# Memory attention and two layers of experts on one core: the prologue rearranged (loads, weight decoding, sums of phi, place of batch 1's attention)

## The chip, the cores and the metric

The kernel runs on one core of a Trainium2 chip. A core has a matrix engine (PE, TensorE), a vector engine (DVE), a scalar engine (ACT), GpSimd (POOL) and a sequencer for DMA issues (SP); each works through its own list of instructions in order, and semaphores tie the lists together. The time is that of one execution on the device, in microseconds (us); the median of three runs counts.

## The reference

```python
# attention with memory: 8 batches, 8 heads, 576 tokens, 64 dims, 32 slots
a = exp(phi - max(phi, axis=2)); a = a / (sum(a, axis=2) + 1e-9)
k_m = einsum('bhsm,bhsd->bhmd', a, k); v_m = einsum('bhsm,bhsd->bhmd', a, v)
scores = q @ k_m^T / sqrt(64)
attn = exp(scores - max(scores)); attn = attn / (sum(attn) + 1e-9)
x = (attn @ v_m), rows of 8 heads x 64            # 4608 x 512
# first layer, weights in float64
h = maximum(maximum(x @ w1, x @ w2), x @ w3)      # 512 -> 768
x = h @ w_out                                     # 768 -> 512
# second layer: of 8 experts the one with the largest logit of x @ w_gate
out = gate_w * (maximum(x @ w1[e], 0) @ w2[e])
```

## The kernel before

The work goes through eight batches. **Attention** of batch b (the `at_` functions) loads phi, k, v and q; takes the maximum of phi over the tokens (`at_max` along the free axis, `at_col` across partitions with a transpose on PE, tile `ps_mx`, then `mc` and `mb`), subtracts it (`at_sub`), takes the exponential on ACT (`at_exp`) and the sum (`at_asum`), and multiplies by k and v on PE (`at_km`, 72 small matmuls, tile `ps_kv`). `kx` and `vx` are the products divided by the sum; `at_kvT` transposes them on PE, `at_qT` transposes q on DVE, `at_scores` makes 32 matmuls, and `at_smax`, `at_sexp`, `at_ssum`, `at_out` are the softmax by halves of the heads (`par`), with the result split into `at_hi` and `at_lo`.

**First layer.** Values are kept as a high part, rounded to the type the fast matmul takes, and the rest: ACT makes the first, DVE or POOL the second (`split`, L94 and L95), and a product is three matmuls (`mm3`, L98 to L100). v_m is folded into the weights: `u_step(b, f)` multiplies a block of `w123` by vT and splits it. `m1_step(b, f, hf, i)` multiplies it by at (6 matmuls of 288 columns); over i, the three products are joined by a maximum `hx` on DVE (L418), and split, `h_lo` on POOL. With 6 f, 2 hf, 3 i these are 216 matmuls in a batch. `m2_step(b, d, hf)` multiplies by w_out, 18 matmuls each, 8 of them in a batch, and needs all six f of h. After it come the gate (`gate_a` to `gate_c`), and at the end, the experts.

**Weights.** The float64 weights of the first layer come in 24 parts (18 of `w123`, 6 of w_out, 128 x 512 words of 8 bytes, 512 KB). `decode_a` takes the upper word's absolute value on ACT (L138) and clamps it (L141); `decode_b` does three bit operations on DVE (L148, L151, L154). A part of w_out is split besides, `wo_lo` on POOL. Parts 0, 1, 2, 8, 11, 15, 22 and 23 are clamped on DVE, the others on POOL. Four raw buffers (`w64`) hold what was loaded.

**Order.** The program is written with a list of times: `attention(b+1)` returns steps with due times (`AT`, and `AT1` for batch 1), and `stream.advance` runs those that are due as m1 and m2 steps of batch b go by; `start_step` decodes the next part in batch 0. A scheduler then fixes the order on each engine. SP issues all loads in one queue in that order. TensorE starts with 34 warm-up matmuls.

Of the kernel before, what the change touches and what calls it, by code (L numbers as in the profile page):

```python
# [19 lines left out]
def kernel(  # L20
# [141 lines left out]
    def w_load(n):  # L162
# [3 lines left out]
        if isinstance(part, tuple):  # L166
            f, i = part
            t = sp.tile([P, J, P], U64, tag="w64", name="w64", bufs=4)
# [27 lines left out]

    def at_max(b):
        t = inp["phi", b]
        mx = ep.tile([P, J, M], F32, tag="mx", name="mx")
        nc.vector.tensor_reduce(out=mx, in_=t.rearrange("p j c m -> p j m c"), axis=AX.X, op=ALU.max)  # L200
        st["mx", b] = mx

    def at_col(b):
# [7 lines left out]
        nc.vector.tensor_copy(out=mb, in_=mc.to_broadcast([P, 2, HP]))  # L211
# [15 lines left out]
    def at_asum(b):  # L227
        t = inp["phi", b]
        asum = ep.tile([P, J, M], F32, tag="mx", name="asum")
        nc.vector.tensor_reduce(out=asum, in_=t.rearrange("p j c m -> p j m c"), axis=AX.X, op=ALU.add)  # L230
        st["asum", b] = asum

    def at_km(b):

        t, kv = inp["phi", b], inp["kv", b]
        pss = [ps_at.tile([P, 512], F32, tag="at", name="ps_kv") for _ in range(2)]
# [11 lines left out]
        for par in range(2):  # L248
# [187 lines left out]

# [330 lines left out]
    with ExitStack():  # L767
        on_dve = (0, 1, 2, 8, 11, 15, 22, 23)

        def w_clamp(n):  # L770
# [4 lines left out]
        load_kv(0, 1)
        w_load(0)
        for j in range(J):
            load_q(0, j)
        w_load(1)
        w_load(2)  # L780
        w_load(3)
        nc.sync.dma_start(out=wg[:, :, 0:E], in_=w_gate.rearrange("(d p) e -> p d e", p=P))
# [17 lines left out]
        w_done(2)  # L800
        w_done(1)
        at_qT(0, 0)
        at_qT(0, 1)
# [1 line left out]
        at_qT(0, 2)
        at_qT(0, 3)
        at_scores(0)
        at_smax(0, 0)
        at_sexp(0, 0)
        w_clamp(3)  # L810
        w_done(3)
        w_clamp(4)
        at_smax(0, 1)
        at_sexp(0, 1)
        at_ssum(0, 1, nc.gpsimd)
        at_ssum(0, 0)
        at_out(0, 0)
        w_done(4)
        at_out(0, 1)
        w_clamp(5)  # L820
# [181 lines left out]
```

## Time and profile before

| | us |
|---|---|
| median of three runs | 1017.89 (1017.39 to 1018.23) |
| the profiled execution | 1020.95 |
| its span | 1019.2 |
| PE busy, DVE, ACT, POOL | 974.2, 580.4, 355.0, 180.5 |
| last at_lo of batch 0 done | 54.6 |
| first matmul of batch 0's m2 | 102.7 |
| first matmul of batch 1's m1 | 130.66 |

The busy times of the engines are sums over the span, which has stages with different limits: the first attention with nothing to hide it, the decoding of the weights beside batch 0's m1, and then seven batches and the experts. So the profile is read by stage. "PEclk" is the clock that was granted to TensorE as a share of full speed (1.0 is 2.4 GHz, 0.5 is 1.2 GHz). A duration in the timeline overlaps the next instruction's by some hundredths of a microsecond, so that the distance from start to start is a little shorter than the duration; for a matmul of 288 columns it is 0.13 where the row says 0.29.

### The profile page before, as it was taken

The page shows a single profiled execution, that of the slowest core. Times are in us where ns is not written, and L with a number is a line of the kernel's source. Part 1 is how long each engine was busy: PE and PEld are TensorE (multiplying, and loading weights), DVE is VectorE, ACT ScalarE, POOL GpSimd, SP SyncE. Part 2 cuts the span into 40 slices and gives each one's busy share as a digit, 9 for nine tenths or more (in the row PEclk, how much of TensorE's full clock was granted, in tenths as well). Part 3 has the DMA queues.
Part 4 walks back from the last instruction along what each step waited for, and adds up shares of the span by engine and source line. Part 5 has one row for each costly group of instructions (what it writes and reads, how often), then busy time and mean ns, then how long its engine had stood idle before and what let it go on. Part 6 is the DMA issues. An engine that isn't in the chain of part 4 may idle for free. (4 is left out here: it accounts for less than half of the span.)

```text
span 1019.2 us, 20430 instructions
## 1 busy us (share of the span) xinstructions
PE 974.2 (96%) x8296; PEld 854.4 (84%) x8296; DVE 580.4 (57%) x1257; ACT 355.0 (35%) x732; POOL 180.5 (18%) x294
## 2 busy tenths in 40 slices
PE   5498899999999999999999999999999999999997
PEld 5176788879888798888989989898989898989886
DVE  5989968385683846838256717171717172626341
ACT  2344433333333434333346406060605050504130
POOL 0124212011120111202121121212121211111110
PEclk7589899999999999999999999999999999999999
DMA  8828214132041321210108517161616161625030
GB/s 313 281 84 277 67 58 161 52 118 70 25 164 48 118 78 37 98 48 2 47 18 267 189 32 223 36 219 41 215 41 201 53 206 51 197 63 155 21 109 22
DMA packets 59105, 114.78 MB, mean 113 GB/s; under 512 B 7687, under 2 KB 20999, under 8 KB 59008
## 3 DMA queue, kind: packets, MB, share of 16 engines
q1 hardware_dynamic: 48480, 94.01, 27.8%
q0 software_dynamic: 4768, 9.94, 4.2%
q10 hardware_dynamic: 5760, 9.48, 2.5%
q8 instruction: 67, 1.10, 0.4%
q14 instruction: 30, 0.25, 0.1%
HBM read 94.00 MB, written 19.44 MB: 111 GB/s over the span
## 5 line engine op out<-in xcount | busy, mean ns | idle before, releaser
L98 PE MATMUL ps_m<-at_hi,u_hi 128*128 128x288 f32 x576 | 178.9, 312 | 3.0 <-DVE hx L418 2.0
L100 PE MATMUL ps_m<-at_hi,u_lo 128*128 128x288 f32 x576 | 170.6, 297 | 2.4 <-DVE u_lo L95 2.4
L99 PE MATMUL ps_m<-at_lo,u_hi 128*128 128x288 f32 x576 | 170.8, 297 | 0.8 <-DVE at_lo L95 0.8
L98 PE MATMUL ps_x<-yh,w1h 128*128 128x288 f32 (+1 forms) x544 | 160.2, 295 | 0.1
L99 PE MATMUL ps_x<-yl,w1h 128*128 128x288 f32 (+1 forms) x544 | 159.9, 294 | 0.0
L100 PE MATMUL ps_x<-yh,w1l 128*128 128x288 f32 (+1 forms) x544 | 159.9, 294 | 0.0
L95 POOL TENSOR_TENSOR h_lo<-hx,h_hi 128x288 fp32r<-128x288 f32 x96 | 83.8, 873 | 375.7 <-ACT h_hi L94 375.6
L98 PEld LDWEIGHTS ps_m<-at_hi,u_hi 128*128 128x128 f32 x576 | 108.6, 189 | 36.6 <-issue 21.5
L596 POOL DMA_DIRECT2D out_dram<-o x144 | 70.9, 499 | 345.6 <-DVE o L593 306.2
L418 DVE TENSOR_TENSOR hx<-hx,ps_m 128x288 f32<-128x288 f32 x192 | 85.2, 446 | 74.5 <-PE ps_m L100 50.6
L98 PE MATMUL ps_m<-h_hi,wo_hi 128*128 128x288 f32 x384 | 115.8, 302 | 1.6 <-ACT wo_hi L94 1.6
L100 PE MATMUL ps_m<-h_hi,wo_lo 128*128 128x288 f32 x384 | 114.1, 298 | 1.3 <-POOL wo_lo L95 1.3
L99 PE MATMUL ps_m<-h_lo,wo_hi 128*128 128x288 f32 x384 | 114.3, 298 | 0.0
L100 PEld LDWEIGHTS ps_m<-at_hi,u_lo 128*128 128x128 f32 x576 | 108.7, 189 | 4.3 <-DVE u_lo L95 3.1
L99 PEld LDWEIGHTS ps_m<-at_lo,u_hi 128*128 128x128 f32 x576 | 109.1, 189 | 2.4 <-issue 1.2
L593 DVE TENSOR_SCALAR o<-ps_x,scal 128x512 f32<-128x512 f32 x32 | 24.0, 751 | 151.6 <-PE ps_x L100 151.6
L98 PE MATMUL ps_x<-w2h,xh 128*128 128x512 f32 x272 | 107.7, 396 | 0.0
L99 PE MATMUL ps_x<-w2l,xh 128*128 128x512 f32 x272 | 107.5, 395 | 0.0
L100 PE MATMUL ps_x<-w2h,xh 128*128 128x512 f32 x272 | 107.4, 395 | 0.0
L98 PEld LDWEIGHTS ps_x<-yh,w1h 128*128 128x128 f32 x544 | 102.0, 188 | 1.4 <-PE ps_g L443 0.5
L99 PEld LDWEIGHTS ps_x<-yl,w1h 128*128 128x128 f32 x544 | 102.1, 188 | 0.5 <-ACT yl L682 0.2
L100 PEld LDWEIGHTS ps_x<-yh,w1l 128*128 128x128 f32 x544 | 102.1, 188 | 0.0
(177 smaller groups left out, 1593.5 us busy)
## 6 DMA issues: line engine op xcount, KB each, us to landing
raw<-in_moe_w_dram SPq DMA_DIRECT2D x72, 512.0 KB, 4.5
raw<-y_dram SPq DMA_DIRECT2D x36, 288.0 KB, 3.1
kv_t<-in_k_dram SPq DMA_DIRECT2D x8, 1152.0 KB, 7.7
kv_t<-in_v_dram SPq DMA_DIRECT2D x8, 1152.0 KB, 9.7
w<-in_moe_w_dram SPq DMA_DIRECT2D x18, 512.0 KB, 4.0
q_t<-in_q_dram SPq DMA_DIRECT2D x32, 288.0 KB, 3.0
y_dram<-y_sb ACTq DMA_DIRECT2D x32, 288.0 KB, 2.1
out_dram<-o POOLq DMA_DIRECT2D x144, 64.0 KB, 1.9
```

What stands on the lines that cost most here:

```text
L95: eng.tensor_tensor(out=dst_lo, in0=src, in1=dst_hi, op=ALU.subtract)
L98: nc.tensor.matmul(out=ps, lhsT=hi_l, rhs=hi_r, start=first, stop=False)
L99: nc.tensor.matmul(out=ps, lhsT=hi_l, rhs=lo_r, start=False, stop=False)
L100: nc.tensor.matmul(out=ps, lhsT=lo_l, rhs=hi_r, start=False, stop=last)
L418: nc.vector.tensor_tensor(out=hx[0], in0=hx[0], in1=ps, op=ALU.max)
L593: nc.vector.tensor_scalar(out=o, in0=ps, scalar1=scal[:, b, t:t + 1], scalar2=None, op0=ALU.mult)
L596: nc.gpsimd.dma_start(out=out5[b, half, c], in_=o[i:i + TB])
```

## The change

- **Loads.** phi, two parts of weights and k go first, then w_gate. The other early loads are tied to a point of the computation by `after`: ACT writes one element of the target from a finished tile, and the load must follow it. w2 and v follow `mb`, w3, the four q and w4 the exponential, two more parts follow `vx`. Six raw buffers in place of four. Part 6 is asked for twice, once by name and once by `w_done(0)`.
- **Decoding.** All clamps on DVE, and `wo_lo` too; of POOL's work in the prologue only `h_lo` stays. `at_ssum`'s product of batch 0 moves to DVE as well.
- **phi.** The maximum, and the sum from batch 2 on, as four tensor_tensor over halves of the chunks (`over_chunks`). The sums of batches 0 and 1 are 72 matmuls against ones. `mb`, `kx` and `vx` are written by ACT.
- **Batch 1's attention** is due late in batch 0 (`AT1`), and its loads follow parts 14, 15 and 17. `start_step` runs at four of six m1 steps.
- **m2 of batch 0, first half**, goes by rows of w_out: four PSUM tiles at once, f as the outer loop. Batch 1's first two `u_step` come in the second half.

```diff
+    NRAW = 6
-    AT1 = dict(max=5, col=8, sub=10, q=(20, 22, 23.5, 25), exp=12.5, asum=13.5, km=24.5, kvT=28.5, sc=31.5,
-               smax=(33, 36), sexp=(36, 38.5), ssum=(37.5, 43), out=(41, 46))
+    AT1 = dict(max=22, col=24, sub=26, q=(24, 25, 26, 27), exp=28, asum=29, km=33, kvT=35, sc=38,
+               smax=(40, 41), sexp=(41, 42.5), ssum=(43, 45), out=(46, 48))
...
+    def after(t, src):
+        nc.scalar.activation(out=t[0:1], in_=src, func=AF.Copy)
...
-        eng.tensor_scalar(out=dst, in0=dst, scalar1=F64_MAX, scalar2=F64_MIN, op0=ALU.min, op1=ALU.max)
+        nc.vector.tensor_scalar(out=dst, in0=dst, scalar1=F64_MAX, scalar2=F64_MIN, op0=ALU.min, op1=ALU.max)
...
-            split(wo_hi[:, part], wo_lo[:, part], wdst[n], nc.gpsimd)
+            split(wo_hi[:, part], wo_lo[:, part], wdst[n])
...
+    def over_chunks(dst, t, op):
+        h = ep.tile([P, J, 4, M], F32, tag="hc", name="hc")
+        nc.vector.tensor_tensor(out=h, in0=t[:, :, 0:4], in1=t[:, :, 4:8], op=op)
+        nc.vector.tensor_tensor(out=h[:, :, 0:2], in0=h[:, :, 0:2], in1=h[:, :, 2:4], op=op)
+        nc.vector.tensor_tensor(out=dst, in0=h[:, :, 0], in1=t[:, :, 8], op=op)
+        nc.vector.tensor_tensor(out=dst, in0=dst, in1=h[:, :, 1], op=op)
...
-        nc.vector.tensor_reduce(out=mx, in_=t.rearrange("p j c m -> p j m c"), axis=AX.X, op=ALU.max)
+        over_chunks(mx, t, ALU.max)
...
-        nc.vector.tensor_copy(out=mb, in_=mc.to_broadcast([P, 2, HP]))
+        nc.scalar.activation(out=mb, in_=mc.to_broadcast([P, 2, HP]), func=AF.Copy)
...
+        if b < 2:
+            pss = st["kvp", b] = [ps_at.tile([P, 512], F32, tag="at", name="ps_kv") for _ in range(2)]
...
+                            lhsT=t[r0:r0 + HP, j, c, :],
+                            rhs=ones[r0:r0 + HP, 0:1],
...
-        nc.vector.tensor_reduce(out=asum, in_=t.rearrange("p j c m -> p j m c"), axis=AX.X, op=ALU.add)
+        over_chunks(asum, t, ALU.add)
...
-            nc.vector.tensor_scalar(out=vx[:, par], in0=ps[:, D:2 * D], scalar1=r, scalar2=None, op0=ALU.mult)
+            nc.scalar.activation(out=vx[:, par], in_=ps[:, D:2 * D], func=AF.Copy, scale=r)
...
+    def m2_by_f(b, hf):
+        pss = [m2_tile(b, d, hf) for d in range(ND)]
+        for f in range(NF1):
+            for d in range(ND):
+                m2_part(b, pss[d], d, hf, f)
+        for d in range(ND):
+            m2_end(b, pss[d], d, hf)
...
-        on_dve = (0, 1, 2, 8, 11, 15, 22, 23)
...
+        w_load(2, st["mb", 0][0:1, 0, 0:1])
+        load_kv(0, 1, st["mb", 0][0:1, 0, 0:1])
...
+        gone = inp["phi", 0][0:1, J - 1, 0, 0:1]
+        w_load(3, gone)
+        for j in range(J):
+            load_q(0, j, gone)
+        w_load(4, gone)
...
+        w_load(5, st["kx", 0][1][0:1, 1, 0:1])
+        w_load(6, st["kx", 0][1][0:1, 1, 0:1])
...
-                stream.add([(0, lambda: load_phi(1)), (20, lambda: load_kv(1, 0)), (21.5, lambda: load_kv(1, 1))])
-                stream.add([(4 + 1.5 * j, lambda j=j: load_q(1, j)) for j in range(J)])
+                stream.add([(16, lambda: load_phi(1, done(14)))])
+                stream.add([(17 + j, lambda j=j: load_q(1, j, done(15))) for j in range(J)])
+                stream.add([(22 + i, lambda i=i: load_kv(1, i, done(17))) for i in range(2)])
...
-                        if b == 0 and (hf, i) in ((0, 0), (1, 0), (1, 2)):
+                        if b == 0 and i != 1:
                             start_step()
...
+                if b == 0 and hf == 0:
+                    m2_by_f(b, hf)
```

**DVE between the first maximum of batch 0 and its subtraction.** `w` is a part of the weights, `qT` a transposed block of q. Before:

```order
L200 TENSOR_REDUCE mx<-phi_t 128x128
L289 STREAM_TRANSPOSE qT<-q_t 128x576 x2
L141 TENSOR_SCALAR w_96<-w_96 128x512
L289 STREAM_TRANSPOSE qT<-q_t 128x576
L148 TENSOR_SCALAR w_96<-w_96 128x512
L289 STREAM_TRANSPOSE qT<-q_t 128x576
L151 SCALAR_TENSOR_TENSOR w_96<-w_153,w_96 128x512
L209 TENSOR_REDUCE mc<-ps_mx 128x2
L154 SCALAR_TENSOR_TENSOR w_96<-w_153,w_96 128x512
L211 COPY mb<-mc 128x128
L141 TENSOR_SCALAR w_96<-w_96 128x512
L218 TENSOR_TENSOR phi_t<-phi_t,ps_mb 128x1152
```

Now (L213 to L216 are the maximum by halves, L152, L159, L162 and L165 what L141, L148, L151 and L154 were):

```order
L215 TENSOR_TENSOR mx<-hc,phi_t 128x128
L216 TENSOR_TENSOR mx<-mx,hc 128x128
L152 TENSOR_SCALAR w_96<-w_96 128x512
L159 TENSOR_SCALAR w_96<-w_96 128x512
L152 TENSOR_SCALAR w_96<-w_96 128x512
L162 SCALAR_TENSOR_TENSOR w_96<-w_150,w_96 128x512
L159 TENSOR_SCALAR w_96<-w_96 128x512
L165 SCALAR_TENSOR_TENSOR w_96<-w_150,w_96 128x512
L162 SCALAR_TENSOR_TENSOR w_96<-w_152,w_96 128x512
L165 SCALAR_TENSOR_TENSOR w_96<-w_152,w_96 128x512
L230 TENSOR_REDUCE mc<-ps_mx 128x2
L239 TENSOR_TENSOR phi_t<-phi_t,ps_mb 128x1152
```

Two parts are decoded ahead of the column maximum `mc`, and nothing stands between it and the subtraction; the four transposes of q come later.

**PE around the end of batch 0's m1.** `ps_kvT` and `ps_sc` are batch 1's transposes and scores, `h_hi,wo_hi` is m2. Before, they stand inside m1:

```order
L98 MATMUL ps_m_1033<-at_hi,u_hi 128x288
L99 MATMUL ps_m_1033<-at_lo,u_hi 128x288
L98 MATMUL ps_m_1052<-at_hi,u_hi 128x288
L99 MATMUL ps_m_1052<-at_lo,u_hi 128x288
L278 MATMUL ps_kvT<-ident,kx 128x128 x2
L279 MATMUL ps_kvT<-ident,vx 128x128
L302 MATMUL ps_sc<-qT,kT 32x288
L100 MATMUL ps_m_1033<-at_hi,u_lo 128x288
L98 MATMUL ps_m_1033<-at_hi,u_hi 128x288
```

Now they stand behind the 72 matmuls of m2 by rows, of which these are the last:

```order
L99 MATMUL ps_m_1265<-h_hi,wo_hi 128x288
L100 MATMUL ps_m_1265<-h_lo,wo_hi 128x288
L101 MATMUL ps_m_1265<-h_hi,wo_lo 128x288
L314 MATMUL ps_kvT<-ident,kx 128x128 x2
L315 MATMUL ps_kvT<-ident,vx 128x128
L99 MATMUL ps_m_1409<-h_hi,wo_hi 128x288
L100 MATMUL ps_m_1409<-h_lo,wo_hi 128x288
L101 MATMUL ps_m_1409<-h_hi,wo_lo 128x288
L99 MATMUL ps_m_1409<-h_hi,wo_hi 128x288
L338 MATMUL ps_sc<-qT,kT 32x288 x32
```

So kvT and scores of batch 1 moved from m1 to behind m2's first half; the sum (L257) and km (L277) stand just ahead of m2.

**PE at batch 1's first m1 block.** Each `ps_m` reads `at_hi` and `at_lo` twice, first for one half of the heads, then for the other. Before:

```order
L100 MATMUL ps_m_1356<-h_hi,wo_lo 128x288
L98 MATMUL ps_m_1377<-at_hi,u_hi 128x288
L99 MATMUL ps_m_1377<-at_lo,u_hi 128x288
L100 MATMUL ps_m_1377<-at_hi,u_lo 128x288
L98 MATMUL ps_m_1377<-at_hi,u_hi 128x288
L99 MATMUL ps_m_1377<-at_lo,u_hi 128x288
L100 MATMUL ps_m_1377<-at_hi,u_lo 128x288
L98 MATMUL ps_m_1390<-at_hi,u_hi 128x288
L99 MATMUL ps_m_1390<-at_lo,u_hi 128x288
```

Now:

```order
L101 MATMUL ps_m_1519<-h_hi,wo_lo 128x288
L99 MATMUL ps_m_1540<-at_hi,u_hi 128x288
L100 MATMUL ps_m_1540<-at_lo,u_hi 128x288
L101 MATMUL ps_m_1540<-at_hi,u_lo 128x288
L99 MATMUL ps_m_1540<-at_hi,u_hi 128x288
L99 MATMUL ps_m_1553<-at_hi,u_hi 128x288
L100 MATMUL ps_m_1553<-at_lo,u_hi 128x288
L101 MATMUL ps_m_1553<-at_hi,u_lo 128x288
L99 MATMUL ps_m_1553<-at_hi,u_hi 128x288
L99 MATMUL ps_m_1567<-at_hi,u_hi 128x288
L100 MATMUL ps_m_1567<-at_lo,u_hi 128x288
L100 MATMUL ps_m_1540<-at_lo,u_hi 128x288
```

The first product with `at_lo` of the second half, `ps_m_1377<-at_lo` the second time and now `ps_m_1540<-at_lo` the second time, was the fifth matmul of the block and is now the eleventh. From the next block on, PE's list is the same in both.

## Rows read from the trace of the kernel before

**Rows 1.** Stages: us, busy (x) PE PEld DVE ACT POOL, PEclk, DMA share, GB/s.

```profile
0.00:12.70 12.70, 9.50 (x69) 9.27 (x69) 2.70 (x13) 1.94 (x2) 0.70 (x6) 1.00 0.86 320
12.70:35.50 22.80, 11.07 (x209) 6.17 (x220) 21.36 (x42) 7.62 (x14) 3.10 (x5) 0.62 0.88 291
35.50:54.60 19.10, 10.27 (x70) 4.46 (x57) 19.08 (x34) 5.95 (x10) 3.22 (x4) 0.50 0.67 233
54.60:102.70 48.10, 43.53 (x482) 33.34 (x481) 44.29 (x83) 22.04 (x47) 19.24 (x22) 0.95 0.59 197
102.70:130.70 28.00, 25.09 (x179) 22.12 (x178) 25.08 (x41) 10.67 (x22) 6.12 (x5) 0.88 0.27 86
130.70:1019.20 888.50, 874.73 (x7307) 779.09 (x7306) 467.92 (x1047) 306.76 (x638) 148.16 (x253) 1.00 0.31 99
```

**Rows 2.** Timeline of PE at batch 1's first m1 block: start us, us, instruction.

```profile
130.53 0.29 PE L100 MATMUL ps_m<-h_hi,wo_lo 128*128 128x288 f32 x1
130.66 0.29 PE L98 MATMUL ps_m<-at_hi,u_hi 128*128 128x288 f32 x1
```

**Rows 3.** Timeline of DVE, phi of batch 0; [idle before <-releaser].

```profile
4.83 2.16 DVE L200 TENSOR_REDUCE mx<-phi_t 128x128 f32<-128x1152 f32 x1 [3.33 <-DMA phi_t<-in_phi_dram]
18.30 1.35 DVE L218 TENSOR_TENSOR phi_t<-phi_t,ps_mb 128x1152 f32<-128x1152 f32 x1 [0.23 <-PE ps_mb L217]
```

**Rows 4.** Timeline of DVE in the weight decoding.

```profile
68.33 0.68 DVE L151 SCALAR_TENSOR_TENSOR w<-w,w 128x512 uint32<-128x512 uint32 x1
68.93 0.44 DVE L418 TENSOR_TENSOR hx<-hx,ps_m 128x288 f32<-128x288 f32 x1
69.29 0.93 DVE L154 SCALAR_TENSOR_TENSOR w<-w,w 128x512 uint32<-128x512 uint32 x1
72.69 0.42 DVE L148 TENSOR_SCALAR w<-w 128x512 uint32<-128x512 uint32 x1
73.49 0.92 DVE L141 TENSOR_SCALAR w<-w 128x512 f32<-128x512 f32 x1
```

**Rows 5.** Timeline of DVE, the last at_lo of batch 0 and of batch 1.

```profile
53.88 0.75 DVE L95 TENSOR_TENSOR at_lo<-aT,at_hi 128x576 fp32r<-128x576 f32 x1
126.50 0.70 DVE L95 TENSOR_TENSOR at_lo<-aT,at_hi 128x576 fp32r<-128x576 f32 x1
```

**Rows 6.** The page's DMA issues: KB each, us from issue to landing.

```profile
w<-in_moe_w_dram SPq DMA_DIRECT2D x18, 512.0 KB, 4.0
```

**Rows 7.** Windows of two microseconds: us, PE busy (x), PEclk, DMA share, GB/s.

```profile
4.00:6.00 2.00, 2.00 (x17) 1.00 1.06 412
104.00:106.00 2.00, 0.59 (x3) 1.00 0.10 39
108.00:110.00 2.00, 1.30 (x6) 0.50 0.00 0
```

**Rows 8.** Timeline of ACT, exp of phi of batch 0.

```profile
19.69 1.26 ACT L225 ACTIVATE phi_t<-phi_t 128x576 f32<-128x576 f32 x2 [1.17 <-DVE phi_t L218]
```

**Rows 9.** Timeline of PE, attention products of batches 0 and 1.

```profile
20.43 4.64 PE L241 MATMUL ps_kv<-kv_t,phi_t 64*32 64x128 f32 x144 [2.16 <-ACT phi_t L225]
29.42 0.66 PE L278 MATMUL ps_kvT<-ident,kx 128*128 128x128 f32 x2 [4.00 <-DVE kx L267]
33.33 4.16 PE L302 MATMUL ps_sc<-qT,kT 32*32 32x288 f32 x62
85.22 1.56 PE L241 MATMUL ps_kv<-kv_t,phi_t 64*32 64x128 f32 x92
98.82 1.45 PE L302 MATMUL ps_sc<-qT,kT 32*32 32x288 f32 x46
```

**Rows 10.** Lines of DVE, 0 to 135: busy us, mean ns | idle before.

```profile
L151 DVE SCALAR_TENSOR_TENSOR w<-w,w 128x512 uint32<-128x512 uint32 x18 | 14.4, 805 | 0.1
```

**Rows 11.** Timeline of POOL beside the clamp at 73.49.

```profile
73.32 0.80 POOL L95 TENSOR_TENSOR h_lo<-hx,h_hi 128x288 fp32r<-128x288 f32 x1 [3.66 <-ACT h_hi L94]
```

**Rows 12.** Waits of PE, 131 to 1020: us, times, longest.

```profile
PE ps_m L98 <- DVE hx L418: 2.0, 6, 0.3
```

More of the change, by code (lines that the diff above doesn't have):

```diff
@@ L160, with w_load @@
     wraw, wdst = {}, {}
-    def w_load(n):
+    def w_load(n, src=None):
         if n >= len(wparts):
@@ L167, in w_load @@
             f, i = part
-            t = sp.tile([P, J, P], U64, tag="w64", name="w64", bufs=4)
+            t = sp.tile([P, J, P], U64, tag="w64", name="w64", bufs=NRAW)
+            if src is not None:
+                after(t.bitcast(F32)[:, 0, 0:1], src)
             nc.sync.dma_start(
@@ L228, in at_asum @@
         t = inp["phi", b]
+        if b < 2:
+            pss = st["kvp", b] = [ps_at.tile([P, 512], F32, tag="at", name="ps_kv") for _ in range(2)]
+            for c in range(NCH):
+                for j in range(J):
+                    for par in range(2):
+                        r0 = HP * par
+                        nc.tensor.matmul(
+                            out=pss[par][32 * j:32 * j + 32, 2 * D:2 * D + 1],
+                            lhsT=t[r0:r0 + HP, j, c, :],
+                            rhs=ones[r0:r0 + HP, 0:1],
+                            start=(c == 0),
+                            stop=(c == NCH - 1),
+                        )
+            return
         asum = ep.tile([P, J, M], F32, tag="mx", name="asum")
-        nc.vector.tensor_reduce(out=asum, in_=t.rearrange("p j c m -> p j m c"), axis=AX.X, op=ALU.add)
+        over_chunks(asum, t, ALU.add)
         st["asum", b] = asum
@@ L235, in at_km @@
         t, kv = inp["phi", b], inp["kv", b]
-        pss = [ps_at.tile([P, 512], F32, tag="at", name="ps_kv") for _ in range(2)]
+        pss = st.pop(("kvp", b)) if b < 2 else [ps_at.tile([P, 512], F32, tag="at", name="ps_kv") for _ in range(2)]
         for c in range(NCH):
@@ L247, in at_km @@
                     )
-        for par in range(2):
+        for par in range(2) if b >= 2 else ():
             r0 = HP * par
@@ L767 @@
     with ExitStack():
-        on_dve = (0, 1, 2, 8, 11, 15, 22, 23)
-        def w_clamp(n):
-            w_a(n, nc.vector if n in on_dve else nc.gpsimd)
         load_phi(0)
+        w_load(0)
+        w_load(1)
         load_kv(0, 0)
[L775 to L782, printed above, removed]
         def w_done(n):
+            w_a(n)
             w_b(n)
-            w_load(n + 4)
+            if n + NRAW < len(wparts) and n + NRAW not in wraw:
+                w_load(n + NRAW)
         at_max(0)
         at_col(0)
+        w_load(2, st["mb", 0][0:1, 0, 0:1])
+        load_kv(0, 1, st["mb", 0][0:1, 0, 0:1])
         at_sub(0)
@@ L793 @@
         at_asum(0)
-        w_clamp(0)
-        w_clamp(1)
+        gone = inp["phi", 0][0:1, J - 1, 0, 0:1]
+        w_load(3, gone)
+        for j in range(J):
+            load_q(0, j, gone)
+        w_load(4, gone)
+        w_done(0)
+        w_done(1)
+        w_done(2)
         at_km(0)
-        w_done(0)
-        w_clamp(2)
+        w_load(5, st["kx", 0][1][0:1, 1, 0:1])
+        w_load(6, st["kx", 0][1][0:1, 1, 0:1])
         at_kvT(0)
[L800 to L803, printed above, removed]
-        u_step(0, 0)
[L805 to L820, printed above, removed]
+        nc.sync.dma_start(out=wg[:, :, 0:E], in_=w_gate.rearrange("(d p) e -> p d e", p=P))
+        for j in range(J):
+            at_qT(0, j)
+        w_done(3)
+        w_done(4)
+        at_scores(0)
+        u_step(0, 0)
+        for p in range(2):
+            at_smax(0, p)
+            at_sexp(0, p)
         w_done(5)
-        w_clamp(7)
-        w_clamp(6)
+        for p in range(2):
+            at_ssum(0, p)
+            at_out(0, p)
         u_step(0, 1)
@@ L872 @@
             for hf in range(2):
+                if b == 0 and hf == 0:
+                    m2_by_f(b, hf)
                 for d in range(ND):
[L874 removed]
+                    if b > 0 or hf > 0:
+                        m2_step(b, d, hf)
                     stream.advance(2.25)
[L876 to L877 removed]
+                    if b + 1 < B and (hf, d) in (((0, 2), (1, 1)) if b else ((1, 1), (1, 2))):
+                        u_step(b + 1, (hf, d) == ((1, 1) if b else (1, 2)))
             stream.rest()
```

61 lines of the change are left out of this document (32 added, 29 removed).

## The prediction

> **What bounds the kernel now.** I read the page's busy shares first, then the windows by stage, then the timelines of single engines inside each stage. TensorE is busy for 974.19 of the 1019.2 us of the span, but not evenly. From 130.70 us on it is busy for 874.73 of 888.50 us at clock 1.00 [rows 1]. Up to there it is not: 12.70 to 54.60 is batch 0's attention, on a half-empty TensorE at a clock of 0.62 and then 0.50, and 54.60 to 130.70 is weight decoding beside batch 0's first products. In these two stages VectorE is the bound: 21.36 of 22.80 us, 19.08 of 19.10, 44.29 of 48.10, 25.08 of 28.00 [rows 1]. The change touches this prologue and little else. In both programs TensorE's order is the same from batch 1's first m1 block to the end, so the result is nearly **one number: when TensorE reaches that block**, 130.66 us before [rows 2].
>
> All sums are in the time of the profiled execution, 1020.95 us, of which 1019.2 is span. It lies 3.06 above the median 1017.89; I add differences to the median. A difference under 0.2%, 2.0 us, can't be told from no change.
>
> **First stage, to the scores of batch 0.** Before, phi's first maximum starts at 4.83 and takes 2.16, but its subtraction only ran at 18.30 [rows 3]: the column maximum stood on VectorE behind a part of a weight and four transposes of q. In the new order these come later. The maximum by halves is four tensor_tensor of 512, 256, 128 and 128 columns. A line through 288 columns (0.36 from start to start) and 576 (0.70 and 0.75 long, about 0.66 from start to start) [rows 4, 5] gives 0.60 + 0.33 + 0.20 + 0.20 = 1.3. ps_mx still waits for the warm-up matmuls, which held TensorE until about 10.6; column maximum, copy (on ScalarE now) and transpose bring the subtraction to about 12.6, 5.7 earlier.
>
> Most of that is lost to transfers. w2 and v are now held back until the copy mb, at about 12.4. A part of a weight lands 4.0 after its issue [rows 6], so w2 at 16.4; v (1152 KB at the 412 GB/s of [rows 7]) lands 2.9 after it, at 19.3. ScalarE's exp, 1.26 for both halves [rows 8], ends at about 15.3. Then come the 72 matmuls against ones that replace the reduction asum. No row has them; the nearest is the km product, 144 passes in 4.64 at half clock, 32 ns each [rows 9]. As many passes cost 4.6, 15.3 to 19.9. Below they could cost a third if one column is cheaper than 128, but then v's landing is next, so the value hardly moves km: it starts at 19.9 and ends at 24.5, where before it ran 20.43 to 25.07. What helps next is the queue on VectorE: kx came 4.00 after TensorE had stopped [rows 9], and it now runs on ScalarE, to about 27.0. Scores then run 28.2 to 32.5 where they ran 33.33 to 37.49 [rows 9]: **5.0 gained**. The softmax of batch 0 and what stands between takes 15.8 on VectorE by the new order (35 instructions, the rows of one price each), against 17.1 before; so the last at_lo ends at T0 = 48.3, before 54.63 [rows 5]: **6.3 gained**. If the scores run at full clock (46 passes in 1.45 instead of 62 in 4.16 [rows 9]), T0 is 46.3.
>
> **Second stage, T0 to phi(1)'s subtraction.** VectorE now does all clamps (16 are left here), wo_lo and phi(1)'s maximum. By its order: 16 clamps at 0.34 = 5.4, 15 L159 at 0.34 = 5.1, 15 L162 and 17 L165 at 0.60 = 19.2 (from start to start in a clean run, 0.42 and 0.68 long [rows 4]), 18 hx at 0.365 = 6.6, six u_lo at 0.47 = 2.8, five wo_lo at 0.60 = 3.0, the maximum 1.3, mc 0.2, the subtraction 1.3, two qT at 0.70 = 1.4: **46.3**.
>
> To this comes contention. Before, L151 took 805 ns on average and 0.68 in the clean run [rows 4, 10], and a clamp that met h_lo on GpSimd took 0.92 instead of 0.42 [rows 4, 11]. Of GpSimd's work only h_lo remains, about nine in this stretch; at 0.35 each 3.2, between 0 and 0.50 each = 4.5. And TensorE's waits come back to VectorE as waits for hx; of the 3.8 idle of before (48.10 - 44.29 [rows 1]) I keep 1.1. So the stage takes 50.6 and the subtraction ends at S = 98.9.
>
> The Trainium skill, "SBUF — State Buffer", section "🔬 SBUF: two separate sides", says of the port pair that VectorE and GpSimd share that it is an exclusive lock: who comes second stands still for the other's whole instruction. The clamp of [rows 4, 11] agrees: 0.92 ends 0.3 after the 0.80 of h_lo does. By that rule nine h_lo could cost 9 x 0.80 = 7.2, and the total would be 4.0 above mine.
>
> **Third stage, S to batch 1's m1.** This is what the change adds. Before, batch 1's attention was spread through the decoding: phi(1)'s sum and km lay among m1 blocks, kvT and the scores too, and all were hidden. Now they stand at the end, in a chain. After S: exp 1.5 [rows 8], 72 matmuls against ones at 17 ns a pass (92 in 1.56 [rows 9]) = 2.45, 32 matmuls of m1 at 0.133 (130.53 to 130.66 [rows 2]) = 4.3, km 2.45: w_out's rows begin at M = S + 10.7 = **109.6**. They began at 102.7 before, but at half clock and with gaps. Then m2 by rows, 72 x 0.133 = 9.6, which stands ahead of kvT on TensorE; kvT 0.5, four matmuls 0.5, scores 64 x 31.5 ns = 2.0. Behind these the softmax of batch 1 on VectorE, with nothing to hide it but the other half of m2: four transposes at 0.40, twelve operations on 576 columns and four qT at 0.68, sums and two u_lo 1.5, exp's latency 0.3 = 14.3. Thus at_lo of the second half is there at M + 26.9 = 136.5, while TensorE's own filler ends at M + 23.5. In the new order the matmul that needs it is the eleventh of batch 1; before, it would have stood at 130.66 + 10 x 0.133 = 132.0. **Lag: 4.5 us.**
>
> **Later batches.** Maximum and sum by halves take 1.3 instead of 2.16 and 2.2; VectorE is not the bound there, but TensorE waits 2.0 for hx in six places [rows 12]. Some of that goes: 0.3 in five batches, 1.5; bounds 0 and 2.0. The moves of mb, kx, vx to ScalarE cost nothing there, since ScalarE is busy for 306.76 of 888.50 [rows 1]. The w_load of part 6 is issued twice, 1.3 us of transfers at 412 GB/s; it delays part 7 on the queue, and six raw buffers cover it.
>
> Forecast: 1017.89 + 4.5 - 1.5 = 1020.9, **1021.0**.
>
> **Rivals.**
> *The prologue sheds its idle time (faster).* Scores at full clock (T0 2.0 earlier), no contention left (3.2), no waits (1.1): M is 103.3, the lag -1.8, and with 2.0 from the later batches the time is 1014; with the softmax tail one or two us shorter, down to 1010.5. For it: VectorE's excess over clean durations was some 7 us in the second stage and GpSimd's part in it goes. Against: h_lo stays, and the clean durations are already in my sum. It decides below M = 105.
>
> *The clock falls in the thin stage (slower).* TensorE's work from T0 to S is 216 matmuls at 0.133 = 28.7 and some 5 for u, of 50.6. Before, a gap at 104 to 106 with 0.59 busy was followed by a clock of 0.50 at 108 to 110, for some microseconds [rows 7]. The stage from 102.70 has a mean clock of 0.88 [rows 1], which over 28.00 us is one spell of some 6.8 at half clock. If such a spell falls on the chain from S to the scores it costs 3.4, twice 6.8: 1024 to 1028, typically 1027. It decides if TensorE idles just ahead of S, while it waits for phi(1). The Trainium skill, "TensorE: Matmul & The Clock Gate", section "HAM oscillation — how this bites in real kernels", has bursts of matmuls divided by waits start each time at the low clock; that speaks against this change, which makes bursts of the chain, and by it the upper of these times would hold.
>
> *What is gained is given back exactly.* The 6.3 of the first stage pay for the tail, M is near 106.3 and nothing can be measured: 1018.
>
> *The lock of the whole instruction* in the second stage (contention 7.2 instead of 3.2): 1025. The row of the clamp bears it out once; most of VectorE's instructions there don't meet an h_lo. I give it 0.08, inside the forecast's share.
>
> **How the numbers follow.** Forecast, with its own range 1017.0 to 1025.0: 0.41 (slower 0.29, same 0.11, faster 0.01). Idle shed: 0.32 (faster 0.31, same 0.01). Clock: 0.19, all slower. Given back: 0.08 (same 0.06, faster 0.01, slower 0.01). Sums: faster 0.33, same 0.18, slower 0.49. The range runs from the far end of the first rival, 1010.5, to beyond the clock's two spells, 1029.5; outside I leave 1 in 10 on either side.
>
> **What would show it.** Right: the subtraction at 12 to 13, scores of batch 0 ended by 33, T0 47 to 49, S near 99, m2's first matmul at 108 to 111, VectorE idle for some 20 us between S and batch 1's scores, a wait of TensorE of about 3 us for at_lo just ahead of batch 1's m1, and that block at 134 to 137. Wrong in the gain: S under 94. Wrong in the clock: granted clock 0.5 anywhere from 85 to 125. Wrong altogether: a shift of batch 1's m1 that is not the shift of the end.

## The result, and the profile after

The changed kernel took 1033.45 us (median of four runs, 1031.11 to 1035.3) beside 1018.06 before: a ratio of **1.0148, interval 1.0122 to 1.0175, slower**. The forecast was 1021.0, range 1010.5 to 1029.5: the right side, and 12 us too low. The profiled execution of the changed kernel has a span of 1033.0, 13.8 more than before.

The stages of the profile after, cut where VectorE begins phi(1)'s subtraction (100.7), where m2 begins (117.2) and where batch 1's m1 begins (142.5); columns as in [rows 1]:

```profile
0.00:12.70 12.70, 9.68 (x70) 9.44 (x70) 6.55 (x25) 3.05 (x5) 0.70 (x6) 1.00 0.67 223
12.70:32.50 19.80, 8.71 (x325) 6.44 (x326) 10.20 (x21) 6.61 (x23) 0.00 (x0) 0.65 0.81 280
...
49.50:100.70 51.20, 37.63 (x236) 28.12 (x234) 48.47 (x100) 22.00 (x52) 11.92 (x8) 0.83 0.62 209
100.70:117.20 16.50, 13.81 (x322) 11.36 (x323) 8.32 (x19) 4.25 (x10) 2.40 (x3) 0.59 0.22 59
117.20:142.50 25.30, 24.32 (x245) 21.01 (x244) 15.49 (x31) 8.55 (x21) 0.80 (x1) 1.00 0.54 188
142.50:1032.00 889.50, 874.44 (x7308) 779.17 (x7306) 458.54 (x1053) 312.56 (x669) 148.64 (x253) 1.00 0.31 99
```

Against [rows 1]: the last stage, to the end of the span at 1033.0, takes 890.5 where it took 888.5, so 11.9 of the 13.8 lie ahead of batch 1's m1, which begins at 142.52 instead of 130.66 [rows 2]. The column of VectorE shows where: it is nearly full from 32.5 to 100.7, and then half empty, 8.32 of 16.50 and 15.49 of 25.30, where before it stayed so to the end (25.08 of 28.00). TensorE stands at a clock of 0.83 and then 0.59.

The first stage gained most of what was forecast. Timelines of VectorE (the subtractions of batch 0 and batch 1, the last two u_lo of batch 0, the last at_lo of batch 1) and of TensorE (km, kvT and scores of batch 0):

```profile
12.99 1.35 DVE L239 TENSOR_TENSOR phi_t<-phi_t,ps_mb 128x1152 f32<-128x1152 f32 x1 [0.77 <-PE ps_mb L238]
100.74 1.34 DVE L239 TENSOR_TENSOR phi_t<-phi_t,ps_mb 128x1152 f32<-128x1152 f32 x1
103.60 0.55 DVE L96 TENSOR_TENSOR u_lo<-ps_u,u_hi 128x384 fp32r<-128x384 f32 x1
104.66 0.55 DVE L96 TENSOR_TENSOR u_lo<-ps_u,u_hi 128x384 fp32r<-128x384 f32 x1
142.53 0.71 DVE L96 TENSOR_TENSOR at_lo<-aT,at_hi 128x576 fp32r<-128x576 f32 x1
```

```profile
19.36 0.65 PE L277 MATMUL ps_kv<-kv_t,phi_t 64*32 64x128 f32 x8 [2.25 <-DMA kv_t<-in_v_dram]
21.14 3.67 PE L277 MATMUL ps_kv<-kv_t,phi_t 64*32 64x128 f32 x128 [1.13 <-issue]
27.61 0.42 PE L277 MATMUL ps_kv<-kv_t,phi_t 64*32 64x128 f32 x8 [2.81 <-issue]
31.39 2.69 PE L338 MATMUL ps_sc<-qT,kT 32*32 32x288 f32 x64 [0.47 <-ACT kT L318]
```

The subtraction runs at 12.99 (before 18.30 [rows 3]), km starts at 19.36 on v's landing as forecast, but its last eight passes come at 27.61, behind a gap for which the profile names no releaser; the scores end at 34.08 (before 37.49 [rows 9]) and the last at_lo of batch 0 at 49.57 (before 54.63 [rows 5]). So 5.1 us are gained here, and 16.9 are lost between there and batch 1's m1.

### The profile page after: what moved, and what is told of

It is laid out like the page before. It is cut to its first block, busy times and chain, and to the rows that moved or that the text cites. A ratio compares the mean times of both kernels' runs of the same rounds, so it can differ in the third digit from the quotient of the medians.

```text
span 1033.0 us, 21090 instructions
## 1 busy us (share of the span) xinstructions
PE 977.6 (95%) x8576; PEld 860.3 (83%) x8576; DVE 564.4 (55%) x1280; ACT 364.5 (35%) x789; POOL 164.5 (16%) x271
## 5 line engine op out<-in xcount | busy, mean ns | idle before, releaser
L99 PE MATMUL ps_m<-at_hi,u_hi 128*128 128x288 f32 x576 | 181.4, 317 | 9.9 <-DVE hx L454 4.1
L101 PE MATMUL ps_m<-at_hi,u_lo 128*128 128x288 f32 x576 | 173.7, 303 | 6.6 <-DVE u_lo L96 5.6
L100 PE MATMUL ps_m<-at_lo,u_hi 128*128 128x288 f32 x576 | 173.3, 302 | 0.0
L96 POOL TENSOR_TENSOR h_lo<-hx,h_hi 128x288 fp32r<-128x288 f32 x96 | 87.7, 914 | 470.2 <-ACT h_hi L95 466.1
L99 PEld LDWEIGHTS ps_m<-at_hi,u_hi 128*128 128x128 f32 x576 | 111.0, 194 | 43.9 <-issue 15.4
L101 PEld LDWEIGHTS ps_m<-at_hi,u_lo 128*128 128x128 f32 x576 | 111.4, 194 | 9.6 <-DVE u_lo L96 7.0
L100 PEld LDWEIGHTS ps_m<-at_lo,u_hi 128*128 128x128 f32 x576 | 111.7, 194 | 0.4 <-DVE at_lo L96 0.3
L99 PE MATMUL ps_x<-w2h,xh 128*128 128x512 f32 x272 | 107.8, 396 | 0.7 <-DVE xh L620 0.7
```

The costliest lines, as they stand in the source:

```text
L96: eng.tensor_tensor(out=dst_lo, in0=src, in1=dst_hi, op=ALU.subtract)
L99: nc.tensor.matmul(out=ps, lhsT=hi_l, rhs=hi_r, start=first, stop=False)
L100: nc.tensor.matmul(out=ps, lhsT=hi_l, rhs=lo_r, start=False, stop=False)
L101: nc.tensor.matmul(out=ps, lhsT=lo_l, rhs=hi_r, start=False, stop=last)
```

## Experiments

The kernel before ran beside each group; its median rose from 1018 to 1021 from the first group to the last, so the ratios to it are what is compared (the changed kernel: 1.0148, 1.0122 to 1.0175).

**First: what TensorE waits for, two parts of the change undone and two things eased.** At 90.9 TensorE stops for 3.27 us, and at 94 its clock has fallen. The chain of that wait, read backwards from TensorE through ScalarE to GpSimd, and VectorE's rows beside it (after; timelines):

```profile
94.16 0.61 PE L99 MATMUL ps_m<-at_hi,u_hi 128*128 128x288 f32 x1 [3.27 <-ACT hx L452]
93.69 0.41 ACT L452 ACTIVATE hx<-ps_m 128x288 f32<-128x288 f32 x1 [2.37 <-POOL h_lo L96]
90.85 2.81 POOL L96 TENSOR_TENSOR h_lo<-hx,h_hi 128x288 fp32r<-128x288 f32 x1 [7.94 <-ACT h_hi L95]
92.60 0.41 DVE L159 TENSOR_SCALAR wod<-wod 128x512 uint32<-128x512 uint32 x1
95.74 0.29 DVE L230 TENSOR_REDUCE mc<-ps_mx 128x2 f32<-128x128 f32 x1 [2.73 <-PE ps_mx L228]
```

h_lo, 0.80 where nothing holds it up (at 101.04), takes 2.81 and ends 0.65 after VectorE's unbroken run of decoding does (93.01). ScalarE's next hx needs that buffer, and TensorE needs ScalarE to empty its PSUM. Four hx buffers cut this chain and leave the order as it is:

```diff
-            hx[0] = lp.tile([P, HS], F32, tag="hx", name="hx", bufs=2)
+            hx[0] = lp.tile([P, HS], F32, tag="hx", name="hx", bufs=4)
```

> The changed kernel with four hx buffers in place of two; the order on every engine stays as it was but for three ScalarE rows and one TensorE row. Theory P (the port): the 3.27 us stall of TensorE at 90.6 to 94.2 comes from h_lo on GpSimd, which took 2.81 us instead of 0.80 while VectorE ran without a pause, and ScalarE's next hx had to wait for it; with more buffers nobody waits for h_lo, the stall goes, the clock doesn't fall at 94 and the chain up to the scores runs at full clock: 5 to 8 us less than 1033.5, some 1026 to 1028. Theory T (the thin stage): TensorE has less work than VectorE in this stretch and idles in any case, the stall only moves and the clock falls all the same: less than 2 us gained.

1029.19, ratio 1.0104 (1.0076 to 1.0132): 4 us gained. The wait for ScalarE's hx is gone though h_lo is as long as before; a wait of 2.56 for VectorE's hx stands at 96.17 in its place, and the clock is down from 95.7 to 109.3 instead of 93.6 to 114.0:

```profile
90.52 2.82 POOL L96 TENSOR_TENSOR h_lo<-hx,h_hi 128x288 fp32r<-128x288 f32 x1 [7.95 <-ACT h_hi L95]
96.17 0.61 PE L99 MATMUL ps_m<-at_hi,u_hi 128*128 128x288 f32 x1 [2.56 <-DVE hx L454]
```

Theory P explains a quarter of the loss; theory T's "the stall only moves" is right for the rest. The same without GpSimd:

```diff
-            split(hs[b, f][0][:, sl], hs[b, f][1][:, sl], hx[0], nc.gpsimd)
+            split(hs[b, f][0][:, sl], hs[b, f][1][:, sl], hx[0], nc.vector if b == 0 else nc.gpsimd)
```

> The changed kernel with h_lo of batch 0 on VectorE, so that GpSimd does nothing in the weight decoding. Theory P: no instruction meets GpSimd any more; VectorE has 12 more of 0.36 us (4.3) and loses the waits of two to three us in all; the long h_lo and the 3.27 us stall go, so the time is 3 to 7 us shorter than 1033.5. Theory T: VectorE's list gets about 2 us longer, TensorE is as thin as before: no gain, 1033 to 1036.

1030.61, 1.0118 (1.0091 to 1.0145): 3 us gained by the medians, hardly clear of the noise, and not in the stage ahead of the subtraction, which still begins at 100.7; TensorE now waits 6.8 for u_lo in two places. Next, batch 1's attention and its loads at their old times:

```diff
-    AT1 = dict(max=22, col=24, sub=26, q=(24, 25, 26, 27), exp=28, asum=29, km=33, kvT=35, sc=38,
...
+    AT1 = dict(max=5, col=8, sub=10, q=(20, 22, 23.5, 25), exp=12.5, asum=13.5, km=24.5, kvT=28.5, sc=31.5,
...
+                stream.add([(0, lambda: load_phi(1)), (20, lambda: load_kv(1, 0)), (21.5, lambda: load_kv(1, 1))])
...
```

> The changed kernel with the due times and loads of batch 1's attention as in the kernel before (its phi, k, v, q loaded early without ties, its attention among the m1 blocks of batch 0). Theory L (late attention): the chain from phi(1)'s subtraction to the last at_lo, 41 us long with VectorE idle for half of it, is what costs; undone, the softmax of batch 1 ends before TensorE's m2 and the time is 10 to 16 us shorter, 1018 to 1023. Theories P and T alone: the half-clock spell stays in the stage ahead and not more than 6 us are gained.

1028.05, 1.0089 (1.0062 to 1.0115): 5 us, half of the least that theory L wanted. This is where the reading of the profile turned: the last at_lo of batch 1 is there at 128.2, 15 us sooner than in the changed kernel, and still m1 of batch 1 begins at 138.8, because m2 of batch 0 only begins at 116.4 (before 102.7). So the late softmax was not the only late thing: batch 0's own m1 is late. Then GpSimd's share of the clamps and wo_lo given back:

```diff
-        decode_a(wdst[n], wraw[n])
+        decode_a(wdst[n], wraw[n], nc.vector if n in (0, 1, 2, 3, 4, 5, 8, 11, 15, 22, 23) else nc.gpsimd)
...
```

> The changed kernel with the clamps of parts 6, 7, 9, 10, 12 to 14 and 16 to 21, and all wo_lo, on GpSimd again. Theory P: more GpSimd work that must fight VectorE for the port, h_lo queues behind it; VectorE has 8 us less of its own work and is held up for 5 or more: gain 0 to 4 us. Theory T: the VectorE-bound stage gets shorter by what it sheds, TensorE is less thin, the clock stays up: gain 5 to 9 us.

1031.34, 1.0120 (1.0092 to 1.0148): 2 us by the medians, inside theory P's 0 to 4 and under theory T's 5 to 9, and not clear of the noise.

**Second: the clock, two parts alone, and what remains.** Extra matmuls of constants into unread columns of m1's PSUM tile fill TensorE's waits:

```diff
+        if b == 0:
+            for _ in range(2):
+                nc.tensor.matmul(out=full[:, HS:HS + P], lhsT=ident, rhs=ones, start=True, stop=True)
...
```

> The changed kernel with two more matmuls behind each m1 block of batch 0, of constants, into columns of the same PSUM tile that nobody reads: 72 of about 0.12 us, 8.8 us of TensorE's time at full clock, laid into the stretch in which it waits. Theory C (the clock itself costs): the granted clock of the changed kernel is 0.5 for some 30 of the 93 us from 49.6 to 142.5; with the gaps filled it stays up, and batch 1's m1 begins 4 to 8 us sooner: 1025 to 1029. Theory D (VectorE's list is the path, TensorE's clock only fills its waits): no gain or a loss, 1032 to 1038.

1030.7, 1.0100 (1.0083 to 1.0117). Windows of TensorE, first the changed kernel, then this one (us, PE busy (x), PEclk, DMA share, GB/s):

```profile
60.00:64.00 4.00, 1.15 (x5) 0.86 0.82 265
64.00:68.00 4.00, 4.00 (x13) 0.50 0.78 246
76.00:80.00 4.00, 4.00 (x31) 0.57 0.99 386
```

```profile
60.00:64.00 4.00, 4.00 (x43) 1.00 0.56 173
64.00:68.00 4.00, 3.58 (x29) 1.00 0.82 239
76.00:80.00 4.00, 3.78 (x30) 1.00 1.00 342
```

The clock now stays at 1.00 from 52 to 98, and the subtraction of phi(1) begins at 100.5 instead of 100.7. So up to there the half clock only filled waits: theory D holds for this stretch, VectorE's list is the path. For the time it doesn't: 3 us less than the changed kernel lies between the two theories. Where they are gained this trace doesn't show: it is of the slowest of the four executions, 1034.4 beside 1029.8 to 1030.8, and in it the clock falls all the same behind the subtraction, from 99.6 to 109.9. In the kernel before, with one part of the change alone:

```diff
-        on_dve = (0, 1, 2, 8, 11, 15, 22, 23)
+        on_dve = tuple(range(24))
...
+            split(wo_hi[:, part], wo_lo[:, part], wdst[n])
```

> The kernel before with one part of the change alone: all clamps and wo_lo on VectorE. Theory P: VectorE gets 16 clamps and six wo_lo more, 9 us, and what is left on GpSimd, h_lo, takes 1.5 to 2.9 us each; 1022 to 1027. Rival: what VectorE sheds in waits for the port pays for it, 1016 to 1020.

1025.19, 1.0049 (1.0032 to 1.0066): 5 us slower, batch 1's m1 at 135.7; but h_lo took 0.79 to 1.37, not the 1.5 to 2.9 that theory P had for it. The size came out as theory P said, the reason did not. And late attention alone, with the new `AT1` and phi, k, v loaded later:

> The kernel before with one part of the change alone: batch 1's attention due late (the new AT1, its phi, k and v loaded later, without ties). Theory L: its softmax stands behind the decoding with nothing to hide it, 1025 to 1030. Rival (the order on VectorE matters little as long as its list is full): 1017 to 1021.

1021.95, 1.0018 (1.0005 to 1.0031): batch 1's m1 at 134.1, but in the time only 0.2%. Theory L's size falls in both directions. Four things at once in the changed kernel: attention early again, the clamps and wo_lo on GpSimd, m2 block by block, four hx buffers:

> The changed kernel with four things undone or eased at once: batch 1's attention early with its loads untied, the clamps of later parts and wo_lo on GpSimd, m2 of batch 0 block by block, four hx buffers. What is left of the change: the new order and ties of batch 0's loads, maximum and sum by halves, the first two sums on TensorE, mb, kx, vx on ScalarE, six raw buffers. If the losses are those of theories P and L, the 3.7 to 5 us gained up to the last at_lo of batch 0 remain: 1012 to 1016, faster than both kernels. If what is left costs too: 1019 to 1025.

1025.81, 1.0054 (1.0036 to 1.0072). Still slower than before, with batch 0's at_lo 3 us sooner and m2 at 116.8: from that at_lo to batch 1's m1 it takes 86.3, before 76.0. Something that all four left in place costs 10 us there.

**Third: the pace.** What was left is the line that calls `start_step`: four parts decoded for each f block of m1 where three were.

```diff
-                        if b == 0 and i != 1:
+                        if b == 0 and (hf, i) in ((0, 0), (1, 0), (1, 2)):
...
```

> The changed kernel with three decoded parts for each f block of batch 0's m1, as before, in place of four (and the ties of batch 1's loads put on parts 12 and 15, since 14 isn't decoded yet). Theory Q (the pace): four parts for each block put a third more decoding ahead of the u_lo and hx for which TensorE waits; at three, the m1 blocks run sooner, w_out is decoded in VectorE's idle time behind phi(1), and the time is 4 to 9 us shorter: 1024 to 1029. Rival (the same work on VectorE in another order ends at the same time): 1031 to 1035.

1022.32, **1.0025 (1.0009 to 1.0040): 11 us gained** by this line and the ties of batch 1's loads that had to move with it; the late attention stays. And the other way round, in the kernel before, where no tie moves:

```diff
-                        if b == 0 and (hf, i) in ((0, 0), (1, 0), (1, 2)):
+                        if b == 0 and i != 1:
```

> The kernel before with one part of the change alone: four decoded parts for each f block in place of three. Theory Q: 1022 to 1028. Rival: within 2 us of 1019.

1031.38, **1.0108 (1.0075 to 1.0140): 11 us lost by the same line**, with nothing else of the change. The mechanism is in VectorE's timeline: where the last u_lo of batch 0 stand, on which the last f block of m1 waits. Kernel before, then b_fast:

```profile
94.06 0.54 DVE L95 TENSOR_TENSOR u_lo<-ps_u,u_hi 128x384 fp32r<-128x384 f32 x1
95.26 0.54 DVE L95 TENSOR_TENSOR u_lo<-ps_u,u_hi 128x384 fp32r<-128x384 f32 x1
```

```profile
106.24 0.55 DVE L95 TENSOR_TENSOR u_lo<-ps_u,u_hi 128x384 fp32r<-128x384 f32 x1
107.31 0.55 DVE L95 TENSOR_TENSOR u_lo<-ps_u,u_hi 128x384 fp32r<-128x384 f32 x1
```

And pace, with phi(1)'s subtraction, against 100.74, 103.60 and 104.66 in the changed kernel:

```profile
89.47 1.35 DVE L239 TENSOR_TENSOR phi_t<-phi_t,ps_mb 128x1152 f32<-128x1152 f32 x1
91.74 0.55 DVE L96 TENSOR_TENSOR u_lo<-ps_u,u_hi 128x384 fp32r<-128x384 f32 x1
92.53 0.55 DVE L96 TENSOR_TENSOR u_lo<-ps_u,u_hi 128x384 fp32r<-128x384 f32 x1
```

Starts read from the timelines, in us:

| | before | b_fast | after | pace |
|---|---|---|---|---|
| last bit operation on a part of `w123` | 89.1 | 84.0 | 78.6 | 84.2 |
| last bit operation on a part of w_out | 114.4 | 107.8 | 104.1 | 110.2 |
| second u_lo of the f block before the last | 83.9 | 91.9 | 85.4 | 78.8 |
| last u_lo of batch 0 | 95.3 | 107.3 | 104.7 | 92.5 |
| last hx of batch 0 | 109.6 | 120.2 | 117.4 | 107.0 |
| first matmul of m2 | 102.7 | 120.0 | 117.2 | 104.7 |
| first matmul of batch 1's m1 | 130.7 | 141.1 | 142.5 | 130.3 |

At four parts a block the decoding ends 6 us **sooner**, and the last u_lo comes 12 us **later**, in both pairs. VectorE does the same work; w_out's parts, wanted only by m2, are done ahead of the splits on which m1 waits, and what is then left to do behind them is TensorE's, with VectorE half empty. The delay grows from block to block: 7 to 8 at the f block before the last, 12 at the last. And it is the place in VectorE's list that holds the split, not its operands: in the changed kernel the product and the high part that the last u_lo (104.66) reads were there by 90.4, with w_out's decoding, among others, between (timeline, after):

```profile
89.05 0.84 PE L424 MATMUL ps_u<-w,vT 64*32 64x384 f32 x6
89.95 0.49 ACT L95 ACTIVATE u_hi<-ps_u 128x384 fp32r<-128x384 f32 x1 [1.12 <-PE ps_u L424]
```

A run that moves these splits alone, at four parts a block, was not made.

**Fourth: combinations at three parts.**

> The combination of the changed kernel with early attention for batch 1, clamps and wo_lo on GpSimd, m2 block by block and four hx buffers, now with three decoded parts for each block as well. Theory Q: the 10 us by which its stretch from the last at_lo of batch 0 to batch 1's m1 was longer than before (86.3 to 76.0) are the pace; 1013 to 1018. Rival (the loss lies in what else is left of the change, such as the sum on TensorE): 1023 to 1027.

1021.94, 1.0015 (0.9997 to 1.0033): 4 us under comb, not the whole of theory Q's size, and batch 1's m1 at 132.8. So in this combination the pace is worth 4 us and not 11; why is not shown.

> The changed kernel with early attention for batch 1, m2 block by block, four hx buffers and three decoded parts for each block, but with all clamps and wo_lo on VectorE as the change has them. If moving the clamps to VectorE costs 5 us, as the kernel before with that part alone showed, this is 4 to 6 us slower than the same combination with the clamps on GpSimd; if the hx buffers take that loss away, equal within 2 us.

1020.94, 1.0005 (0.9987 to 1.0022), no slower than with the clamps on GpSimd. In this combination the place of the clamps doesn't matter; why it costs 5 us in the kernel before stays open.

**Fifth: the clock on the chain behind the subtraction, and the buffers.**

```diff
+        for _ in range(20 if b == 1 else 0):
+            nc.tensor.matmul(out=ps[:, P:2 * P], lhsT=ident, rhs=ones, start=True, stop=True)
...
```

> The changed kernel with four hx buffers and extra matmuls of constants, which nobody reads, in the stretch ahead of batch 1's sum: two behind each m1 block of the last two f, twenty behind the transpose of mb. Beside hx4 (1029.2; subtraction of phi(1) at 98.0, first matmul of m2 at 113.5, half clock from 95 to 108.7). If the half clock costs the chain what its rows say, 32 matmuls at 0.24 instead of 0.133, m2 begins 2 to 4 us sooner after the subtraction (12 us instead of 15.5) and the time is 1025 to 1027. If the clock only fills waits there as well, the distance stays at 15 and the time at 1028 to 1031.

1029.79, 1.0096 (1.0068 to 1.0124), no gain over hx4: inconclusive, since the clock fell all the same from 102.5 to 109.3, after a wait of 2.2 for exp.

> The changed kernel with three decoded parts for each block and four hx buffers. With the pace undone, fewer h_lo are held up; if the buffers still matter as in the changed kernel (4 us), 1017 to 1019; if the long h_lo were an effect of the pace, no gain over pace: 1021 to 1023.

1019.66, 0.9994 (0.9982 to 1.0007): 2 to 3 us under pace, between the two expectations; some h_lo are still long (1.99, 3.16, 2.77), so they don't follow from the pace. It has the lowest ratio of all and equals the kernel before. The 5 us of the first stage (at_lo of batch 0 at 49.5 in pace, 54.6 before) are lost again ahead of batch 1's m1 (130.3 and 130.7); where, no run separates.

> pace_hx4 with the extra matmuls of constants, behind the m1 blocks of the last three f and behind the transpose of mb. Pace has half clock from 89.5 to 100, all on the chain from phi(1)'s subtraction to m2. If that is worth what the rows say, 2 to 4 us under pace_hx4 and for the first time under the kernel before; else within 1.5 us of pace_hx4.

1024.94, 1.0042 (1.0024 to 1.0061): slower, but it shows what the clock is worth on this chain. Its windows (columns as above):

```profile
90.00:94.00 4.00, 4.00 (x158) 1.00 0.98 372
94.00:98.00 4.00, 4.00 (x62) 1.00 0.08 29
98.00:102.00 4.00, 4.00 (x161) 1.00 0.01 4
```

At full clock the chain from the subtraction's end (91.5) to m2 (103.4) takes 11.9, beside 13.3 in pace_hx4, which has half clock from 92.0 to 98.8, and 13.9 in pace, from 89.9 to 100.1. So such a spell costs this chain 1.4 to 2. What made the total worse is a wait of TensorE for VectorE's hx of 3.4, up to 108.2, which pace_hx4 doesn't have; how the extra matmuls bring it about was not followed.

Not tried: the second load of part 6, m2 by rows by itself, the sums of phi on TensorE by themselves, and six raw buffers by themselves.

## Why the prediction was wrong, step by step

Two steps failed. "M = S + 10.7" took 15.2: TensorE's work behind the subtraction was priced without a gap and at full clock, and it ran at half clock. And the third stage's "this is what the change adds", the late attention, is not where the loss comes from: late attention alone cost 0.2%, the pace alone 1.1%. That the forecast was on the right side is in part luck: its wait for at_lo, from which the lag was worked out, did not occur.

- **First stage.** Right in its mechanism: subtraction at 12.99 (12.6 forecast), the gain lost again to v's landing, kx by ScalarE. The matmuls against ones took 1.7, not 4.6, so that v's landing and not they set km's start. T0 was 49.57 for 48.3: the late passes of km (27.61 for an end at 24.5) cost 3, the scores at a higher clock (64 passes in 2.69) gave back 1.6.
- **Second stage.** T0 to the end of the subtraction took 52.5 (49.57 to 102.08) for 50.6. The sum of VectorE's instructions and the price of contention held: VectorE was busy for 49.8, 3.5 over the 46.3, where 3.2 were forecast. Seven instructions that met an h_lo make up the 3.5, as here (after):

```profile
81.92 0.98 POOL L96 TENSOR_TENSOR h_lo<-hx,h_hi 128x288 fp32r<-128x288 f32 x1 [3.53 <-ACT h_hi L95]
82.16 1.03 DVE L159 TENSOR_SCALAR wod<-wod 128x512 uint32<-128x512 uint32 x1
```

  What was too small is the term for TensorE's waits that come back: 1.1 was kept, and VectorE waited 2.73, once, at 95.74, for TensorE that had waited for a long h_lo. The rule of the exclusive lock (the Trainium skill, "SBUF — State Buffer", section "🔬 SBUF: two separate sides") agrees with the row at 82.16, which ends 0.3 after its h_lo does; the 7.2 that the prediction worked out from it did not come, and the loser was at times GpSimd, whose h_lo took 2.91 and 2.81.
- **Third stage: the term that failed.** "M = S + 10.7" was 15.2 (102.08 to 117.25). TensorE idled for 3.27 just ahead, ran at half clock from 93.6 to 114.0, and the m1 matmuls took 0.24 from start to start:

```profile
92.00:94.00 2.00, 0.00 (x0) 0.90 0.00 0
94.00:96.00 2.00, 1.84 (x7) 0.50 0.00 0
112.00:114.00 2.00, 2.00 (x11) 0.50 0.00 0
114.00:116.00 2.00, 2.00 (x128) 0.98 0.00 0
```

```profile
109.27 0.44 PE L100 MATMUL ps_m<-at_lo,u_hi 128*128 128x288 f32 x1
109.51 0.44 PE L101 MATMUL ps_m<-at_hi,u_lo 128*128 128x288 f32 x1
114.26 2.15 PE L277 MATMUL ps_kv<-kv_t,phi_t 64*32 64x128 f32 x130
117.25 0.29 PE L99 MATMUL ps_m<-h_hi,wo_hi 128*128 128x288 f32 x1
```

  26 of the 32 at 0.24 instead of 0.133 make 2.8 of the 4.5, an estimate from these rows; pace_swarm, on a shorter spell, has 1.4 to 2. The rest is gaps, such as one of 0.94 at 107.76 for which the profile names no releaser, and is not split further. This is the rival on the clock, with its place as written (TensorE idle just ahead of S); it had 0.19, where the profile before already showed such a fall behind a gap (m2 stood there at full clock, 1.00 at 104 to 106 [rows 7], and fell only behind the gap; the prediction has it at half clock from its start).
- **The lag** at the matmul that wants at_lo was 11.9 for 4.5. At_lo of the second half came 26.0 after M (26.9 forecast), at 143.24, and TensorE reached that matmul only at about 143.8: the forecast wait of some 3 us for at_lo did not occur. What TensorE had to do set the time: its own list took 25.3 from M to batch 1's m1 for 23.5, with a wait for u_lo in m2's second half:

```profile
139.72 0.85 PE L424 MATMUL ps_u<-w,vT 64*32 64x384 f32 x8 [0.98 <-DVE u_lo L96]
142.52 0.29 PE L99 MATMUL ps_m<-at_hi,u_hi 128*128 128x288 f32 x1
```

  By that list alone the forecast's lag was 2.4 (133.1 for 130.66); M came 7.7 later (1.3, 1.9 and 4.5 from the three stages), and the list took 1.8 more: 11.9.
- **Later batches.** The gain of 1.5 didn't come; the stage took 1.9 more. The waits for hx of [rows 12] are gone, but those of TensorE for the scores' transposes grew (waits of PE: before, 131 to 1020, and after, 140 to 1033):

```profile
PE ps_u L388 <- DVE sc L310: 1.7, 4, 0.5
```

```profile
PE ps_u L424 <- DVE sc L346: 3.7, 5, 1.0
```

  From batch 1's m1 to the end, kernels with the halves took 885.9 to 891.0 and the kernel before with and without single parts 887.6 to 891.1: no difference beyond their spread. The 12.4 by which the forecast was low are thus 7.4 of the lag, 3.4 here, and 1.6 by which the medians differ more than the two spans.
- **The part that was passed over.** The order on VectorE was priced as it stood, but the line that made it, four parts a block, was not weighed as an edit, and late attention got the blame in the forecast's third stage. At three parts, with attention as late as the change has it, the time was 0.25% over the kernel before (pace), and equal to it with more hx buffers (pace_hx4). Undoing late attention at four parts still gained 5 us (att1), so the two are not independent. Asked of the order alone, the question "which rows stand ahead of the last u_lo" would have shown it: w_out's decoding, which nobody on m1's path needs.
- **What would make it wrong** was named rightly (granted clock 0.5 between 85 and 125). By the runs the clock is worth 1.4 to 2.8 of the missing 12, not all of them.

## What to carry to other kernels

When preparation (decoding, conversion, loading ahead) shares a bound engine with the work that feeds the next engine, its pace is an edit of its own: find the last instruction that the next engine waits for and count what stands ahead of it that isn't needed yet. Finishing the preparation sooner is a loss if it moves that instruction back. A change with many parts is best split by running single parts in both directions; here two parts undone and two things eased in the changed kernel gave 2 to 5 us each, and the pace gave 11.

## What the runs showed that was not expected

- A GpSimd tensor_tensor of 128x288 with operands in SBUF, 0.80 us alone, took 2.81, 2.91 and up to 4.0 us (swarm) beside an unbroken run of VectorE's shifts, clamps and two-operand bit operations, and the first two ended some 0.65 after that run did (at 93.01, where VectorE paused, and at 62.97, where a u_lo from PSUM came next). The other way round, a shift of VectorE's that came second took 1.03 instead of 0.42. That a shared port is what held them is argued from the times and from the rule of the Trainium skill ("SBUF — State Buffer", section "🔬 SBUF: two separate sides"), not shown by itself.
- Half clock on TensorE did not move the end of a stretch in which VectorE's list was the path: two spells at 0.5 in the changed kernel, around 66 and 78 us, ran at 1.00 in warm2, and the start of the subtraction moved by 0.2 us.
